# Another table of places for the steps of a fused attention and bilinear feed-forward kernel

## The chip, the cores and the metric

One core of a Trainium2 chip. The metric is the device time of one execution in microseconds (us), the median of several runs; lower is better. The engines are TensorE (PE; its weight loads are shown as PEld), VectorE (DVE), ScalarE (ACT), GpSimd (POOL) and SyncE (SP), which here issues all the transfers. Every engine works through its own queue in the order in which the program was written; semaphores hold an instruction back until what it needs is there, and then everything behind it in that queue waits too.

## The reference

The input x has 2048 rows of 576 numbers; all is float32.

```python
xn = layernorm(x)
qkv = xn @ wqkv                       # 32 heads of 18
s = softmax(mask(q k^T / sqrt(18))) v # a row sees itself and the 255 rows before it
s = concat(s) @ wo
g = silu(((xn @ w_gate) * (xn @ w_up)) @ w_down)   # inner width 4608
return x + s * g
```

## The kernel before

All products run on TensorE in float16, each operand split in a high and a low half (three products in place of one, high-high, high-low, low-high), so "hi" steps (ACT casts), "lo" steps (DVE or POOL subtract) and sums of them make up most of the work of the other engines.

**Before slot 0** (the first 180 us): layernorm, the transposed input XT, then the projections to q, k and v, which go to DRAM.

**The slots.** The feed-forward's inner width is cut into 18 groups g of 256, each worked in four slots: 72 slots in all (`NSLOT`). Slot `4g + 2c + kind` computes gate (kind 0) or up (kind 1) of group g for half c of the rows, by a scheme with seven half-size products in place of eight (`seven_place`, line 1184, PSUM banks named `up`). The seven are taken in the order `ORDER = (0, 2, 1, 3, 4, 5, 6)` and called q0 to q6. Each is read out of its bank by ACT (`seven_copy`, line 1148) or by DVE (`seven_add`, line 1157; `seven_fuse`, line 1151). There are two banks: q1 goes on in q0's after that was read, q3 in q2's, q5 in q3's, q6 in q4's, and the next slot's q0 and q2 take the banks of q5 and q6. So a late read holds TensorE. The scheme needs sums of input blocks (`s_steps`: tiles SX, XD and one block of XT rewritten in place, once at the start) and of weight blocks (`t_sum`, tile `tw`, for each group), all split in halves again.

**Places.** A slot has 16 places; `SEVEN_N` says how many of the 46 products of line 1184 each place has. Between them the program puts all other steps: `at(slot, place, f, ...)` files a step, and after the products of a place its steps are written out in the order in which they were filed (score products first, then `down`). The table `AT` holds the places. A place above 15 lies in the next slot: place 24 of slot 45 is place 8 of slot 46. Negative places lie before slot 0.

**The steps of attention.** There are 64 steps s, each two heads (j) for 512 rows in four blocks of 128 (i). Step s begins in slot b = s + 1 and takes row `b % 4` of the tables `p`, `end` and `en`. For each of n = 2i + j, `AT['p'][b % 4][n]` has five places:

```python
for n in range(8):
    i, j = divmod(n, 2)
    for f, p in zip((score, shifted, probs, turn_probs, weigh), AT["p"][b % NCH][n]):
        at(b, p, f, s, j, i)
at(b, AT["end"][b % NCH][0], finish, s)
at(b, AT["end"][b % NCH][1], finish2, s)
```

- `score` (line 931, DVE): mask and row maximum of a block of scores; the scores themselves are TensorE's (`score_pairs`, line 920, at places 6 and 13).
- `shifted` (line 939, ACT, at j = 1): the factor for the exponent.
- `probs` (lines 943 and 946, ACT): the exponential, and at j = 1 the high halves of both heads in tile `pp`.
- `turn_probs` (line 952): the low half, on DVE where `AT['en'][b % 4][2 + 2i + j]` is 1 and on POOL where it is 0. At j = 1 SP then issues the transposing transfer pp -> pt (line 955) for both heads of the block. Tile pt has three buffers.
- `weigh` (line 964, TensorE): the six products of P and V of one head and block, reading pt into the bank `pv`. The first of the two heads waits for the transfer.
- `finish` (lines 976 and 977, DVE) reads the bank `pv` after the last `weigh` of the step; `finish2` (lines 984 to 992, POOL) scales and splits it; `store_o` sends it to DRAM.

**The other steps of a slot.** `h_hi` and `h_lo` (lines 1025 and 1031, ACT and DVE, places `AT['h']`) split gate times up, in four tiles gv, gt, g and gu; the buffer of gt is taken by the next q0 read, which therefore waits for `h_lo` of gt. `down` (line 1046, bank `dn`, one bank; evicted by DVE, line 1053) is the product with w_down. `ffn_raw`, `ffn_amax` (line 321, ACT), `ffn_spread_*`, `up_hi`/`up_lo`, `dn_*`, `t_*`, `wd_*` load, scale and split the next group's weights. `load_q`, `load_k`, `load_v` (`AT['load']`) fetch the next step's q, k and v. The tables `sx`, `on`, `t0`, `u0`, `g0`, `wd0` place the sums and weight steps of the first group, before and in slots 0 to 2; `on` chooses DVE (1) or POOL (0) for each sum.

**After slot 71** the output projection and the combination with x run in 16 tiles (`o_out`, line 1292).

In what follows a slot's kind is its number modulo 4 (slot 46 is of kind 2), and row r of a table is that of the steps that begin in a slot of kind r.

Of the kernel before, what the change touches and what calls it, by code (L numbers as in the profile page):

```python
# [20 lines left out]
def kernel(  # L21
# [43 lines left out]
    C_OUT = 1.0 / (XS * PROJ * WTOP * WTOP)  # L65
    LEAST, MOST = 2.0 ** -60, 2.0 ** 60

    AT = {'amax': (19, 30, 6),
          'dn': ((45, 45), (48, 55), (54, 49)),
          'down': ((6, 9, 12, 16, 20), (6, 8, 11, 19, 16), (6, 8, 11, 14, 16), (6, 10, 12, 15, 18)),  # L70
          'down_last': ((11, 11, 12, 13, 11), (2, 3, 4, 5, 9)),
          'en': ((0, 1, 0, 0, 0, 0, 1, 1, 0, 0), (0, 1, 0, 0, 0, 1, 1, 0, 0, 0), (1, 1, 0, 0, 0, 0, 1, 1, 0, 0),
                 (0, 1, 0, 0, 0, 0, 0, 1, 0, 0)),
          'end': ((31, 32, 35), (29, 32, 33), (28, 32, 33), (28, 32, 33)),
          'eng': (1, 1, 1, 1, 1, 0, 1, 0, 1, 0, 0, 0, 0, 1),
          'g0': (-22, -17, -22, -18, -10, -16, -14, -11, -11),
          'h': (((17, 20), (15, 16), (17, 21), (19, 20)), ((13, 14), (16, 16), (16, 18), (19, 20))),
          'h_last': ((17, 18), (18, 19)),
          'load': (8, 10, 15),
          'me': (0, 1, 0),  # L80
          'mult': {4: 1, 5: 1, 6: 1},
# [12 lines left out]
          'pairs': (6, 13),  # L94
          'raw': (8, 10, 21, 22, -8, 0),
          'scale': (30, 31, 38, 50),
          'sum': ((46, 52, 55, 56), (64, 66, 67, 70)),
# [5 lines left out]
          't_hi': ((57, 70), (61, 74)),  # L103
          't_lo': ((59, 73), (70, 77)),
          'u0': ((-9, -2, -7, -3), (-7, -2, -6, 3)),
          'up_hi': (41, 54, 45, 60),
          'up_lo': (44, 57, 50, 65),
          'wd': ((58, 72), (65, 73), (71, 78)),
          'wd0': ((-4, 6), (-1, 6), (2, 17))}

    ctx.enter_context(tc.manual_schedule())
    const = ctx.enter_context(tc.tile_pool(name="const", bufs=1))
# [512 lines left out]
    def dn_low(g, k):  # L625
        w = DW[g, k]
        if AT["eng"][4]:
            nc.scalar.activation(w[:, 2], w[:, 0], AF.Copy, scale=1.0 / LO)
# [22 lines left out]
    def at(slot, place, f, *a):  # L651
        todo.setdefault(slot * 16 + place, []).append((f, a))
# [5 lines left out]
    for c in range(NCH):  # L658
        steps = s_steps(c)
        for n, f in enumerate(steps):  # L660
            for k, f in enumerate(f if isinstance(f, tuple) else (f,)):
                at(0, AT["sx"][c][n] + k, f, (nc.gpsimd, nc.vector)[AT["on"][c][n]])
    for k in range(3):
        at(0, AT["g0"][k], ffn_amax, 0, (2, 0, 1)[k])
    for k, f in enumerate((ffn_spread_out, ffn_spread_in, ffn_scale, ffn_scale2)):
        at(0, AT["g0"][5 + k], f, 0)
    for kind in range(2):
        for n in range(4):
            at(0, AT["t0"][kind][n], t_sum, 0, kind, n)
        for pair in range(2):  # L670
            at(0, AT["t0"][kind][4 + pair], t_hi, 0, kind, pair)
            at(0, AT["t0"][kind][6 + pair], t_lo, 0, kind, pair)
# [682 lines left out]
```

## Time and profile before

| what | value |
|---|---|
| runs before | 1584.62 us median of 3 (1583.49 to 1588.78) |
| the profiled execution | 1583.03 us, its span 1581.2 us |
| granted TensorE clock | 1.0 |
| busy: PE, DVE, ACT, POOL | 1549.4, 1267.6, 1047.0, 761.7 us |
| slot 0 begins | 179.53 us after the span's start |
| the last slot begins | 1492.76 us |

The views used below: the page of the whole execution, the list of waits (who waited for whom, in total), the chain of work that ended last in order of time (start, duration, what), and timelines of one engine in a window (start, duration, engine, line, operation, out<-in, shape, count, and in brackets the idle time before it with what ended it). In a timeline equal instructions that follow each other are one row, and the duration of PE rows runs past the next row's start, since matmuls are pipelined and their ends are modelled.

### The profile page before, as it was taken

The page shows a single profiled execution, that of the slowest core. Times are in us where ns is not written, and L with a number is a line of the kernel's source. Part 1 is how long each engine was busy: PE and PEld are TensorE (multiplying, and loading weights), DVE is VectorE, ACT ScalarE, POOL GpSimd, SP SyncE. Part 2 cuts the span into 40 slices and gives each one's busy share as a digit, 9 for nine tenths or more (in the row PEclk, how much of TensorE's full clock was granted, in tenths as well). Part 3 has the DMA queues.
Part 4 walks back from the last instruction along what each step waited for, and adds up shares of the span by engine and source line. Part 5 has one row for each costly group of instructions (what it writes and reads, how often), then busy time and mean ns, then how long its engine had stood idle before and what let it go on. Part 6 is the DMA issues. An engine that isn't in the chain of part 4 may idle for free.

```text
span 1581.2 us, 32793 instructions
## 1 busy us (share of the span) xinstructions
PE 1549.4 (98%) x11898; PEld 769.9 (49%) x11898; DVE 1267.6 (80%) x2803; ACT 1047.0 (66%) x1818; POOL 761.7 (48%) x985
## 2 busy tenths in 40 slices
PE   8999999999999999999999999999999999999999
PEld 5465444444444444444444444444444444444467
DVE  7636788888888989898989898888988888967654
ACT  6534587767777877777877777777877777842130
POOL 4115445545464646464646555655656465622000
PEclk9999999999999999999999999999999999999999
DMA  8683456566557786777777777777786777641238
GB/s 222 208 237 128 147 99 122 107 120 112 110 106 141 129 148 132 140 131 139 138 134 140 130 145 133 145 124 147 136 138 134 135 128 151 126 88 36 65 84 217
DMA packets 566546, 211.67 MB, mean 134 GB/s; under 512 B 504560, under 2 KB 544624, under 8 KB 566384
## 3 DMA queue, kind: packets, MB, share of 16 engines
q1 hardware_dynamic: 566384, 209.58, 65.6%
q8 instruction: 93, 1.52, 0.4%
q14 instruction: 69, 0.57, 0.1%
HBM read 76.63 MB, written 29.00 MB: 67 GB/s over the span
## 4 chain that ended last, share of the span: by engine, by line
PE 73%; DVE 11%; DMA 6%; issue 3%; ACT 2%; POOL 2%; SPq 1%; DVEq 0%; ACTq 0%; POOLq 0%
PE up L1184 33%; PE dn L1046 18%; DMA pt<-pp 5%; PE pv L964 4%; PE s L393 4%; DVE hh L1031 3%; PE up L1134 2%; PE s L1046 2%; PE s L1292 2%; PE s L920 2%; PE up L1292 2%; PE up L393 1%; DVE gt L1160 1%; DVE acc L1053 1%; PE pv L393 1%
## 5 line engine op out<-in xcount | busy, mean ns | idle before, releaser
L1046 PE MATMUL dn<-dnw,hh 128*128 128x512 f16 (+1 forms) x3168 | 442.5, 286 | 0.0
L1046 PEld LDWEIGHTS <-hh 128*128 128x128 f16 x3456 | 222.9, 98 | 224.1 <-issue 21.1
L1053 DVE SCALAR_TENSOR_TENSOR acc<-dn,sc,acc 128x512 f32<-128x512 f32 x310 | 215.3, 694 | 84.2 <-PE dn L1046 82.2
L939 ACT ACTIVATE mx<-mx,sig 128x2 f32<-128x2 f32 x256 | 98.4, 384 | 240.7 <-DVE mx L931 239.5
L1184 PE MATMUL up<-XT,upw 128*128 128x512 f16 x936 | 238.8, 379 | 5.2 <-ACT gt L1148 5.0
L1184 PE MATMUL up<-XT,tw 128*128 128x512 f16 x864 | 232.3, 378 | 4.2 <-DVE gu L1157 1.4
L1184 PE MATMUL up<-sx,tw 128*128 128x512 f16 x864 | 222.9, 378 | 0.1
L1184 PEld LDWEIGHTS <-tw 128*128 128x128 f16 x1728 | 147.4, 97 | 142.6 <-issue 9.1
L519 POOL TENSOR_TENSOR raw<-raw 128x256 f32<-128x256 f32 x140 | 125.1, 894 | 72.6 <-DVE upw L199 63.5
L964 PEld LDWEIGHTS <-pt 128*128 128x128 f16 x2880 | 115.1, 96 | 88.4 <-DMA pt<-pp 22.1
L1184 PEld LDWEIGHTS <-upw 128*128 128x128 f16 x936 | 86.6, 98 | 102.6 <-issue 10.4
L964 PE MATMUL pv<-vt,pt 128*128 128x37 f16 x2880 | 120.5, 179 | 11.4 <-DMA pt<-pp 11.2
L1184 PE MATMUL up<-sx,upv 128*128 128x512 f16 x432 | 111.3, 381 | 0.0
L1160 POOL TENSOR_TENSOR gv<-gv,uv 128x512 f32<-128x512 f32 x36 | 53.5, 1487 | 62.4 <-DVE uv L1157 62.4
L1184 PEld LDWEIGHTS <-upv 128*128 128x128 f16 x576 | 49.2, 97 | 69.4 <-issue 22.1
L321 ACT ACTIVATE upw<-raw 128x1280 bf16<-128x1280 f32 (+1 forms) x51 | 62.3, 1221 | 9.8 <-DMA raw<-in_B_w_up_dram 9.1
L920 PE MATMUL s<-ks,qs 54*128 54x384 f16 (+2 forms) x512 | 60.2, 312 | 0.0
L199 DVE SCALAR_TENSOR_TENSOR tw<-raw,sc,tw 128x512 f16<-128x512 f32 x70 | 57.1, 816 | 0.0
L1160 POOL TENSOR_TENSOR gu<-gu,uu 128x512 f32<-128x512 f32 x36 | 47.5, 1320 | 19.6 <-DVE uu L1157 14.8
L984 POOL TENSOR_TENSOR o<-o,rc 128x144 f32<-128x144 f32 x64 | 29.7, 465 | 56.4 <-DVE o L977 56.4
L1157 DVE SCALAR_TENSOR_TENSOR uu<-up,ut 128x512 f32<-128x512 f32 x36 | 24.9, 692 | 39.6 <-PE up L1134 21.6
L1134 PE MATMUL up<-XT,upv 64*128 64x512 f16 x144 | 55.7, 386 | 0.1
(1356 smaller groups left out, 3234.5 us busy)
## 6 DMA issues: line engine op xcount, KB each, us to landing
raw<-in_B_w_down_dram SPq DMA_DIRECT2D x36, 288.0 KB
qk_d<-qp SPq DMA_DIRECT2D x18, 512.0 KB
raw<-in_B_w_gate_dram SPq DMA_DIRECT2D x36, 256.0 KB
raw<-in_B_w_up_dram SPq DMA_DIRECT2D x36, 256.0 KB
ks<-qk_d SPq DMA_DIRECT2D x96, 81.0 KB
qs<-qk_d SPq DMA_DIRECT2D x128, 54.0 KB
vt<-v_d SPq DMA_DIRECT2D x48, 111.0 KB
qk_d<-qp SPq DMA_DIRECT2D x20, 256.0 KB
```

What stands on the lines that cost most here:

```text
L321: nc.scalar.activation(to[0:src.shape[0], 0:src.shape[-1]], src, AF.Square, accum_out=dst)
L393: nc.tensor.matmul(ps, a, b, start=i == 0 and not opened, stop=i == 12 and opened)
L519: nc.gpsimd.tensor_tensor(to, x0, x1, op=OP.subtract)
L920: nc.tensor.matmul(ps[:, :hi_ - lo_], QS[s][r, i * 128:(i + 1) * 128], KS[s][r, lo_:hi_], start=True, stop=True)
L939: nc.scalar.activation(mx[:, 1], mx[:, 0], AF.Identity, bias=sig[:, 2:3], scale=sig[:, 1:2])
L964: nc.tensor.matmul(PVB[s][:, j, i, :VW], pt[:, nb * j + n + n // nb * nb], VT[s][:, lo_ + n % nb, j * VW:(j + 1) * VW], start=n == 0, stop ...
L1046: nc.tensor.matmul(to, a, b, start=q == 0, stop=q == len(l) - 1)
L1053: nc.vector.scalar_tensor_tensor(d, src, SC[g][:, 9:10], d, op0=OP.mult, op1=OP.add)
L1134: nc.tensor.matmul(CH[q], w, x, start=False, stop=s, skip_group_check=q in ON)
L1160: eng.tensor_tensor(GT[name], GT[name], SV[name], op=OP.mult)
L1184: nc.tensor.matmul(CH[q], a, b, start=CH["first"], stop=last and q not in (1, 2, 5), skip_group_check=q in ON)
L1292: nc.tensor.matmul(pr[j][:, :cols[j].stop - cols[j].start], a, b[:, cols[j]], start=i == 0, stop=i == 13)
```

## The change

Only the table `AT` differs; no step is added or removed. In `p` the places of `weigh` move, with some of `score`, `shifted`, `probs` and `turn_probs` ahead of them; `en` gives one low half in row 0 to POOL and one to DVE, and one in row 1 to POOL; in row 3 `finish` and `finish2` move by two and one places; `load_q` goes three places ahead; some `h`, `up_hi`, `wd`, `t_hi` and `amax` steps move by one to four places; the steps of the first group (`sx`, `on`, `t0`, `u0`, `g0`, `wd0`) get new places and engines, and so do the last slot's `h_last` and `down_last`. Entry 8 of `eng` is read nowhere.

```diff
-    AT = {'amax': (19, 30, 6),
+    AT = {'amax': (21, 30, 6),
...
-          'down_last': ((11, 11, 12, 13, 11), (2, 3, 4, 5, 9)),
-          'en': ((0, 1, 0, 0, 0, 0, 1, 1, 0, 0), (0, 1, 0, 0, 0, 1, 1, 0, 0, 0), (1, 1, 0, 0, 0, 0, 1, 1, 0, 0),
+          'down_last': ((9, 11, 13, 13, 13), (2, 2, 3, 5, 6)),
+          'en': ((0, 1, 0, 0, 0, 0, 0, 1, 0, 1), (1, 1, 0, 0, 0, 0, 1, 0, 0, 0), (1, 1, 0, 0, 0, 0, 1, 1, 0, 0),
                  (0, 1, 0, 0, 0, 0, 0, 1, 0, 0)),
-          'end': ((31, 32, 35), (29, 32, 33), (28, 32, 33), (28, 32, 33)),
-          'eng': (1, 1, 1, 1, 1, 0, 1, 0, 1, 0, 0, 0, 0, 1),
-          'g0': (-22, -17, -22, -18, -10, -16, -14, -11, -11),
-          'h': (((17, 20), (15, 16), (17, 21), (19, 20)), ((13, 14), (16, 16), (16, 18), (19, 20))),
-          'h_last': ((17, 18), (18, 19)),
-          'load': (8, 10, 15),
+          'end': ((31, 32, 35), (29, 32, 33), (28, 32, 33), (30, 33, 33)),
+          'eng': (1, 1, 1, 1, 1, 0, 1, 0, 0, 0, 0, 0, 0, 1),
+          'g0': (-22, -17, -22, -17, -12, -15, -14, -12, -11),
+          'h': (((17, 19), (15, 15), (17, 21), (18, 19)), ((13, 14), (16, 16), (16, 21), (19, 21))),
+          'h_last': ((17, 18), (19, 19)),
+          'load': (8, 7, 15),
...
-          'on': ((0, 0, 0, 1, 1, 1, 1, 1, 0, 1, 0, 0, 0, 0, 1, 0, 1),
-                 (0, 0, 0, 1, 1, 0, 0, 0, 0, 0, 1, 0, 1, 1, 0, 0, 1),
-                 (1, 1, 0, 1, 0, 0, 1, 0, 0, 0, 1, 1, 1, 0, 1, 1, 1),
-                 (0, 0, 1, 0, 0, 0, 0, 1, 0, 0, 1, 1, 1, 1, 0, 1, 1)),
-          'p': (((6, 7, 8, 11, 21), (6, 7, 10, 12, 22), (7, 8, 9, 13, 22), (7, 8, 10, 13, 23), (13, 14, 15, 18, 24),
-                 (13, 14, 15, 18, 24), (13, 15, 20, 21, 30), (15, 17, 20, 21, 30)),
-                ((6, 7, 8, 11, 22), (6, 7, 8, 12, 25), (7, 8, 12, 13, 22), (8, 8, 12, 15, 23), (13, 14, 15, 18, 24),
-                 (13, 14, 16, 20, 24), (17, 17, 20, 21, 27), (17, 17, 20, 21, 28)),
-                ((6, 6, 7, 8, 22), (6, 6, 7, 10, 22), (7, 9, 14, 15, 22), (7, 9, 14, 15, 23), (13, 15, 15, 17, 26),
-                 (13, 14, 15, 19, 26), (14, 15, 20, 21, 28), (15, 17, 20, 21, 28)),
-                ((6, 7, 8, 11, 22), (6, 7, 8, 12, 22), (7, 8, 12, 13, 22), (7, 8, 12, 13, 23), (13, 14, 15, 19, 26),
-                 (13, 14, 15, 21, 26), (13, 17, 20, 21, 28), (15, 17, 20, 21, 28))),
+          'on': ((0, 0, 0, 1, 0, 1, 1, 1, 0, 0, 0, 0, 0, 1, 1, 0, 1),
+                 (0, 0, 1, 1, 1, 0, 0, 0, 1, 0, 1, 0, 1, 1, 0, 1, 1),
+                 (1, 1, 1, 1, 0, 0, 1, 0, 0, 0, 1, 1, 1, 0, 1, 1, 0),
+                 (0, 1, 1, 0, 0, 0, 0, 0, 0, 0, 1, 0, 0, 1, 0, 1, 0)),
+          'p': (((6, 7, 8, 11, 22), (6, 7, 10, 13, 22), (6, 8, 9, 13, 23), (7, 8, 10, 13, 23), (13, 13, 14, 17, 27),
+                 (13, 13, 14, 18, 27), (13, 18, 21, 22, 30), (18, 18, 21, 22, 30)),
+                ((6, 7, 8, 11, 22), (6, 7, 10, 12, 22), (7, 10, 12, 15, 22), (10, 10, 14, 15, 23), (13, 15, 16, 18, 26),
+                 (13, 15, 16, 20, 26), (16, 18, 19, 20, 28), (17, 18, 19, 20, 28)),
+                ((6, 6, 7, 8, 22), (6, 6, 7, 12, 22), (7, 8, 14, 15, 22), (7, 8, 14, 15, 23), (13, 14, 15, 17, 26),
+                 (13, 14, 15, 19, 26), (14, 17, 18, 21, 28), (15, 17, 18, 21, 28)),
+                ((6, 7, 8, 11, 20), (6, 7, 8, 12, 20), (7, 8, 12, 13, 22), (7, 8, 12, 13, 22), (13, 14, 15, 19, 26),
+                 (13, 14, 15, 21, 26), (13, 17, 20, 21, 30), (17, 17, 20, 21, 30))),
...
-          'sx': ((-24, -24, -24, -23, -22, -22, -18, -18, -17, -17, -14, -13, -13, -20, -20, -17, -14),
-                 (-21, -21, -21, -18, -17, -17, -16, -14, -14, -11, -10, -10, -9, -15, -15, -15, -12),
-                 (-14, -11, -11, -10, -7, -7, -4, -3, 2, 3, 6, 6, 6, 2, 17, 17, 18),
-                 (-4, -2, -1, 5, 8, 12, 12, 14, 14, 16, 20, 26, 27, 23, 26, 26, 30)),
-          't0': ((-19, -9, -7, -7, -6, -6, -4, -3), (0, 2, 4, 6, 5, 11, 9, 11)),
-          't_hi': ((57, 70), (61, 74)),
+          'sx': ((-24, -22, -22, -22, -21, -21, -18, -15, -15, -15, -14, -14, -13, -20, -19, -17, -14),
+                 (-21, -21, -21, -20, -17, -17, -16, -14, -14, -14, -13, -12, -9, -16, -15, -12, -12),
+                 (-14, -8, -8, -8, -7, -7, -4, -3, -3, 2, 6, 6, 6, -1, 15, 20, 20),
+                 (-2, -1, -1, 5, 8, 12, 12, 14, 16, 19, 23, 35, 38, 25, 26, 33, 35)),
+          't0': ((-20, -9, -7, -7, -6, -6, -4, -3), (0, 2, 5, 6, 5, 11, 9, 15)),
+          't_hi': ((57, 70), (59, 75)),
...
-          'u0': ((-9, -2, -7, -3), (-7, -2, -6, 3)),
-          'up_hi': (41, 54, 45, 60),
+          'u0': ((-9, -2, -9, -3), (-7, -2, -6, -2)),
+          'up_hi': (39, 54, 47, 60),
...
-          'wd': ((58, 72), (65, 73), (71, 78)),
-          'wd0': ((-4, 6), (-1, 6), (2, 17))}
+          'wd': ((58, 72), (66, 77), (72, 78)),
+          'wd0': ((-4, 6), (-1, 6), (5, 19))}
```

## The prediction

> **What bounds the kernel now.** I read the page first, then the list of waits, then the chain of work that ended last, and then timelines around the waits.
>
> ```profile
> span 1581.2 us, 32793 instructions
> PE 1549.4 (98%) x11898; PEld 769.9 (49%) x11898; DVE 1267.6 (80%) x2803; ACT 1047.0 (66%) x1818; POOL 761.7 (48%) x985
> PEclk9999999999999999999999999999999999999999
> ```
>
> TensorE is busy 98% of the span at the full granted clock, and its work does not change. So the change can only fill, or open, holes in TensorE's queue. The list of waits names them:
>
> ```profile
> PE pv L964 <- DMA pt<-pp: 11.2, 15, 2.3
> PE up L1184 <- ACT gt L1148: 5.0, 17, 1.6
> ```
>
> Products of P and V wait 11.2 us, in 15 places, for the transposing transfer. The chain gives the same from another side. Every fourth slot has the same stretch of 18 products, so their distances are periods of four slots (start, duration, what):
>
> ```profile
> 522.60 3.89 PE up L1184 x18
> ...
> 749.70 3.88 PE up L1184 x18
> 824.35 3.88 PE up L1184 x18
> ...
> 1354.95 3.88 PE up L1184 x18
> ```
>
> From 522.60 to 1354.95 lie 11 periods, 75.67 us each; one without such a wait takes 824.35 - 749.70 = 74.65. Eleven times 1.02 is 11.2 us: in the middle of the kernel the variable part is these waits.
>
> **Term 1: `weigh` in row 1.** The timeline of PE in slot 46 (kind 2), and the two largest rows of their sort:
>
> ```profile
> 1041.18 0.47 PE L964 MATMUL pv<-vt,pt 128*128 128x37 f16 x12 [0.42 <-DMA pt<-pp]
> 1041.49 0.59 PE L1184 MATMUL up<-XT,tw 128*128 128x512 f16 x2
> 1041.92 0.38 PE L1184 MATMUL up<-sx,tw 128*128 128x512 f16 x1
> 1042.30 1.24 PE L1184 MATMUL up<-sx,tw 128*128 128x512 f16 x5
> ...
> 890.78 0.47 PE L964 MATMUL pv<-vt,pt 128*128 128x37 f16 x12 [1.72 <-DMA pt<-pp]
> 1269.96 0.47 PE L964 MATMUL pv<-vt,pt 128*128 128x37 f16 x12 [2.28 <-DMA pt<-pp]
> ```
>
> The first is block 2 of a step of row 1: low half at place 20, product at 24, four places apart, the closest pair of the table. It moves to 26. What then lies between is the rest of place 8, the three products of place 9 and the two of place 10: five products, 0.216 us each (3.88/18), so 1.08 us later. The bracket understates a hole by about 0.16 us, because the 0.38 us of a product run past its 0.216. The waits outside kind 0 sum to 8.2 us in ten rows by their brackets (11.2 less the 3.0 of term 2), 9.8 with the 0.16 each. Left over are what exceeds 1.08: 0.8 and 1.36 of the two largest, some 0.1 of the next, 2.3 in all. Term 1 is -7.5 (0 if the transfer comes later by as much, -9.8 if none is left). Does it come later? POOL gets one more low half in row 1 (i1, j1), but ahead of `finish2`, for which POOL waits anyway; the transfer itself follows POOL's (i2, j1), whose predecessors are as before. Block 3 leaves place 27 for 28. Its transfer stands behind block 2's in SP's queue and needs a buffer of pt, freed at place 22 by block 0 (25 before); `store_o` and the loads behind it gain, and `load_q`, which passes `load_k` and one `ffn_raw` on that queue, finds its buffer free since the slot before. Both at nothing.
>
> **Term 2: `weigh` in row 3, block 2.** Its places stay, 21 and 26, five apart; what changes is DVE's queue ahead of the low half.
>
> ```profile
> 1156.05 0.47 PE L964 MATMUL pv<-vt,pt 128*128 128x37 f16 x12 [0.99 <-DMA pt<-pp]
> 1073.17 1.01 DVE L1031 SCALAR_TENSOR_TENSOR hh<-hh,g 128x512 f16<-128x512 f16 x1
> 1074.10 1.21 DVE L1031 SCALAR_TENSOR_TENSOR hh<-hh,gu 128x512 f16<-128x512 f16 x1
> 1075.23 0.55 DVE L952 TENSOR_TENSOR pp<-sm__14852,pp 128x384 f16<-128x384 f32 x1
> 1075.85 3.27 SPq L955 DMA_TRANSPOSE pt<-pp  x2
> ```
>
> SP issues right after DVE's low half, and the two `h_lo` (g, gu) that stood ahead of it go behind: 1075.23 - 1073.17 = 2.06 us earlier. The largest wait of this sort is the 0.99 shown; five of them, 0.16 to 0.99, sum to 3.0 by brackets, 3.8 with the 0.16. Term 2 is -3.8 (0 to -3.8). The delayed `h_lo` feed `down` a slot later: nothing.
>
> **Term 3: the q0 read in kind 0.** Nearly all of the 17 waits for ACT gt are in slots of kind 0, such as slot 48:
>
> ```profile
> 1070.53 0.54 DVE L931 CUSTOM_DVE_ANT_0 sm__14856<-s,bias 128x384 f32<-128x384 f32 x1
> 1071.00 0.85 DVE L1031 SCALAR_TENSOR_TENSOR hh<-hh,gt 128x512 f16<-128x512 f16 x1
> 1071.94 0.60 ACT L1148 ACTIVATE gt<-up 128x512 f32<-128x512 f32 x1 [1.05 <-DVE hh L1031]
> 1072.59 1.67 PE L1184 MATMUL up<-XT,upw 128*128 128x512 f16 x7 [0.22 <-ACT gt L1148]
> ...
> 1080.15 0.69 DVE L1157 SCALAR_TENSOR_TENSOR gv<-up,gt 128x512 f32<-128x512 f32 x1
> 1080.95 1.03 PE L1184 MATMUL up<-XT,tw 128*128 128x512 f16 x4
> ```
>
> The `score` ahead of `h_lo` of gt moves behind it, 0.54 us, more than the 0.22 + 0.16 waited. But DVE has no idle time from here to the read at 1080.15, whose end at 1080.84 releases q5 at 1080.95, and up to that read it does the same steps in another order. What q1 gains, q5 waits: -0.5 in all (0 to 12 x 0.38 = -4.6).
>
> **Term 4: `finish` in row 3, against the change.**
>
> ```profile
> 1083.97 0.20 DVE L976 RECIPROCAL rc<-pv 128x8 f32<-128x8 f32 x1
> 1084.58 0.69 DVE L1157 SCALAR_TENSOR_TENSOR gt<-up,gt 128x512 f32<-128x512 f32 x1
> 1088.11 0.69 DVE L1157 SCALAR_TENSOR_TENSOR gu<-up,gu 128x512 f32<-128x512 f32 x1
> 1088.91 1.46 PE L1184 MATMUL up<-sx,tw 128*128 128x512 f16 x6
> ```
>
> Now `finish` (0.61 us, 1083.97 to 1084.58) fills the time in which DVE would wait for q5, whose products end at about the same moment. At place 30 it follows the q5 read, ahead of the q6 read, and that one's end (1088.80) releases q2 of the next slot at 1088.91. Three scores, two low halves and the read lie between without idle time, so the read comes up to 0.6 us later. Two of these DVE steps now run beside `finish2` on POOL, which will come later too; I take 0.35 per group in the 12 groups from slot 20 on and a trifle before: +4.3 (0 to 16 x 0.6 = +9.6). ACT's `wd_hi` of 0.39 us ahead of the exponentials there meets idle time.
>
> The Trainium skill ("SBUF — State Buffer", Who interferes with whom) says that a DVE instruction with two SBUF inputs and a GpSimd one that reads SBUF exclude each other for a whole instruction. The `h_lo` row of 1.21 us in term 2 agrees, against this one beside an idle POOL:
>
> ```profile
> 1036.55 0.68 DVE L1031 SCALAR_TENSOR_TENSOR hh<-hh,g 128x512 f16<-128x512 f16 x1
> ```
>
> By that rule the new order in term 3's stretch could cost or save one such difference, 0.5 us, in each group, 6 us either way; the sum takes none.
>
> **Term 5: slots 0 to 2.** The waits of PE from 179 to 226 us:
>
> ```profile
> PE up L1184 <- ACT gt L1148: 1.6, 1, 1.6
> PE up L1184 <- DVE gu L1157: 1.4, 2, 0.9
> PE up L1184 <- DVE uu L1157: 1.2, 1, 1.2
> PE up L1184 <- DVE gv L1157: 1.1, 1, 1.1
> ...
> 183.40 0.61 DVE L199 SCALAR_TENSOR_TENSOR upv<-raw,sc,upv 128x384 f16<-128x384 f32 x1
> 208.02 1.49 DVE L952 TENSOR_TENSOR pp<-sm__2061,pp 128x256 f16<-128x256 f32 x1
> ```
>
> With two of 0.2 that is 5.7 us, nearly all for DVE's reads. DVE loses the `up_lo` of 0.61 (now before slot 0, where it idles) and the low half of 1.49 (to POOL), and a sum. Against that the third block of the first sums (z, split at places 35 and 36) is needed by q3 at 39, and its tail goes out at 39 for place 45. I take -2.5 (-6 to +3). The earlier places before slot 0 meet a TensorE that waits for almost nothing there, and the last slot's new places move products within a full queue: nothing.
>
> The rest is covered: `up_hi`, `wd_hi`, `t_hi` and `amax` move by a few places to where their results are needed later still, and row 0's last low half on DVE (place 22) has its product at 30.
>
> **The sum.** -7.5 - 3.8 - 0.5 + 4.3 - 2.5 = -10.0 us. From the profiled execution's 1583.0 (its span of 1581.2 and 1.8 around it) that is 1573.0; the median of the runs is 1.6 above that execution, which I leave inside the range.
>
> **Rivals.**
>
> *More of it, 1567.* `finish` falls into a pause (term 4 at 0) and the early slots gain more: -7.5 - 3.8 - 0.5 - 4 = -16. For it: groups with a wait of term 2 have slack before that q2 now. Against it: no idle bracket in term 4's DVE rows.
>
> *The waits move on, 1583.* The transfers come as much later as the products: block 2's of row 1 needs POOL, and SP may stand at a transfer that waits for its buffer. Then terms 1 and 2 shrink to -3, term 4 stays. Against it: the order on POOL and SP. The table also does not do all that its name says: block 2 of row 3 keeps five places, of row 1 gets six; were term 2 alone missing, the time would be 1577, within the forecast.
>
> *Slower, 1591: ACT holds q1 in kind 2.* Row 1's exponentials go from places 12 and 15 to 14 and 16, right ahead of the q0 read at place 17.
>
> ```profile
> 1029.26 0.39 ACT L939 ACTIVATE mx<-mx,sig 128x2 f32<-128x2 f32 x1 [2.57 <-DVE mx L931]
> 1033.39 0.59 ACT L1148 ACTIVATE gt<-up 128x512 f32<-128x512 f32 x1
> 1034.42 1.67 PE L1184 MATMUL up<-XT,upw 128*128 128x512 f16 x7
> ```
>
> That read ends at 1033.98, 0.44 us ahead of q1. Were it 1.5 us later, as long as a moved exponential with its copy, 1.06 us would be lost in each of 17 slots, 18 us: +8. It decides from 0.44 + 10/17 = 1.0 us on. Against it: ACT idles 2.57 us just before, and `amax`, which now follows that row, can go into that gap.
>
> **How the numbers follow.** Forecast 0.51 (1573, own range 1568 to 1578), more of it 0.18, waits move on 0.20, slower 0.11. The range is 1563 to 1585: below by what terms 3 and 5 could add, above to the waits that move on; the slower rival and the outer tails stay out. A change under 0.3% (4.8 us; the runs shown span 5.3) can't be told from none: faster 0.72 from the first two and a little of the third, same 0.17, slower 0.11.
>
> **What the next profile would show.** Term 1: waits of pv for the transfer under 3 us, periods of four slots under 75.2. Term 2: none in kind 0. Term 3: the waits for ACT gt gone, q5 at the end of DVE's read. Term 4: a new row, PE up waits for DVE's q6 read in slots of kind 1, about 0.3 us each. Term 5: under 4 us of waits before 226 us. I would be wrong if a wait for ACT appeared in kind 2, or if the pv waits stood as they are.

## The result and the profile after

| kernel | runs | median us (range) | ratio to before, 95% interval |
|---|---|---|---|
| before | 4 | 1586.16 (1583.49 to 1588.78) | |
| changed | 4 | 1574.11 (1572.70 to 1575.38) | 0.9924 [0.9902, 0.9946] |

The change is 12.0 us faster by the medians. The two profiled executions lie closer together, 1583.03 and 1575.38 us: that of before lies below all four of its runs, that of the changed kernel is the highest of its four. Of the 46 runs of the kernel before that stand beside the experiments, the 22 with a granted clock of 1.0 have a median of 1582.8 us and the 24 with 0.997 to 0.999 one of 1586.7, while all four runs of the changed kernel had 1.0. Like for like the change is thus worth 8 to 9 us, near the difference of the two profiled executions, which both had 1.0. The page of the changed kernel, which answers to the first rows of the prediction:

```profile
span 1573.3 us, 32759 instructions
...
PE 1550.6 (99%) x11898; PEld 770.8 (49%) x11898; DVE 1273.1 (81%) x2790; ACT 1050.7 (67%) x1818; POOL 759.4 (48%) x998
...
PEclk9999999999999999999999999999999999999999
```

TensorE's work is the same and its clock too, so the 7.9 us by which the span is shorter are holes. The list of waits (us in total, times, longest):

```profile
PE up L1184 <- ACT gt L1148: 4.5, 17, 1.1
PE pv L964 <- DMA pt<-pp: 2.9, 4, 1.1
PE up L1184 <- DVE gu L1157: 2.7, 8, 0.9
```

The products of P and V wait 2.9 us where they waited 11.2. The row of 5.0 us for ACT's read of gt has hardly moved (its 0.5 us are one early wait, 1.6 to 1.1), and the row for DVE's reads into gu, 1.4 us before, has grown. The chain, with the same stretch of 18 products once in four slots:

```profile
518.51 3.88 PE up L1184 x18
...
668.48 3.88 PE up L1184 x18
743.59 3.88 PE up L1184 x18
818.44 3.88 PE up L1184 x18
...
1346.86 3.88 PE up L1184 x18
```

Eleven periods are 828.35 us, 75.30 each (75.67 before). But one without a wait for a transfer is now 74.85 (818.44 - 743.59) or 75.11 (743.59 - 668.48), where it was 74.65. So something was paid for the gain. Last, the waits of TensorE from 179 to 226 us:

```profile
PE up L1184 <- DVE gu L1157: 1.7, 2, 0.9
PE up L1184 <- ACT gt L1148: 1.1, 1, 1.1
PE up L1184 <- DVE uu L1157: 0.6, 1, 0.6
PE up L1184 <- DVE gv L1157: 0.4, 1, 0.4
```

For the accounts below a wait is measured as the distance from the start of one product to that of the next, less the usual distance of that pair; this sees the 0.16 us that the brackets leave out. By the starts of slots, the span changed by -2.3 us up to slot 4, by -1.8 from slot 4 to 20, by -4.0 from slot 20 to 64, by +0.5 from there to slot 71 and by -0.3 after it: -7.9. The -4.0 of the middle are, for slots 20 to 63, three numbers: waits for transfers 11.2 to 3.0 us, new waits for the q3 read ahead of q5 at place 12 of kind 0 (+2.1), and for the q6 read at place 2 of kind 1 (+2.2).

### The profile page after: what moved, and what is told of

It reads as the page before. It is cut to its first block, busy times and chain, and to the rows that moved or that the text cites. A ratio compares the mean times of both kernels' runs of the same rounds, so it can differ in the third digit from the quotient of the medians.

```text
span 1573.3 us, 32759 instructions
## 1 busy us (share of the span) xinstructions
PE 1550.6 (99%) x11898; PEld 770.8 (49%) x11898; DVE 1273.1 (81%) x2790; ACT 1050.7 (67%) x1818; POOL 759.4 (48%) x998
## 4 chain that ended last, share of the span: by engine, by line
PE 70%; DVE 9%; POOL 8%; issue 6%; ACT 3%; DMA 2%; SPq 0%; DVEq 0%; POOLq 0%; ACTq 0%
PE up L1184 32%; PE dn L1046 18%; POOL pp L952 4%; PE pv L964 3%; PE s L393 3%; PE up L1134 2%; PE s L1046 2%; DVE hh L1031 2%; DMA pt<-pp 2%; PE s L1292 2%; PE s L920 2%; PE up L1292 2%; PE up L393 1%; POOL raw L519 1%; DVE gt L1160 1%
## 5 line engine op out<-in xcount | busy, mean ns | idle before, releaser
L1184 PEld LDWEIGHTS <-tw 128*128 128x128 f16 x1728 | 152.0, 97 | 161.7 <-issue 14.6
L519 POOL TENSOR_TENSOR raw<-raw 128x256 f32<-128x256 f32 x140 | 121.4, 867 | 57.1 <-DVE upw L199 48.2
L964 PEld LDWEIGHTS <-pt 128*128 128x128 f16 x2880 | 109.3, 96 | 64.9 <-DMA pt<-pp 5.8
L964 PE MATMUL pv<-vt,pt 128*128 128x37 f16 x2880 | 112.9, 180 | 2.9 <-DMA pt<-pp 2.9
L984 POOL TENSOR_TENSOR o<-o,rc 128x144 f32<-128x144 f32 x64 | 34.4, 537 | 71.2 <-DVE o L977 71.2
L1134 PE MATMUL up<-XT,upw 64*128 64x512 f16 x144 | 55.7, 387 | 0.0
```

The source lines that it names most:

```text
L519: nc.gpsimd.tensor_tensor(to, x0, x1, op=OP.subtract)
L964: nc.tensor.matmul(PVB[s][:, j, i, :VW], pt[:, nb * j + n + n // nb * nb], VT[s][:, lo_ + n % nb, j * VW:(j + 1) * VW], start=n == 0, stop ...
L1134: nc.tensor.matmul(CH[q], w, x, start=False, stop=s, skip_group_check=q in ON)
L1184: nc.tensor.matmul(CH[q], a, b, start=CH["first"], stop=last and q not in (1, 2, 5), skip_group_check=q in ON)
```

## Experiments

All times below are medians of six runs (eight for the second), each set beside runs of the kernel before on the same chip; four chips were used, so kernels of different groups are compared by their ratios and by their traces, and a difference of medians between such kernels is only a rough figure. Each ratio holds the difference of clock named above. An interval of a ratio is some 0.0036 wide, 5.7 us; what is smaller rests on the waits in the traces.

| kernel | median us (range) | ratio to before, 95% interval |
|---|---|---|
| row 1 weigh alone | 1576.99 (1575.03 to 1578.49) | 0.9943 [0.9926, 0.9960] |
| row 3 low halves alone | 1579.98 (1578.53 to 1583.11) | 0.9972 [0.9954, 0.9990] |
| changed, finish back | 1571.20 (1570.16 to 1571.74) | 0.9906 [0.9890, 0.9922] |
| changed, old start | 1576.71 (1575.09 to 1578.85) | 0.9944 [0.9925, 0.9963] |
| changed, row 1 block 2 at 28 | 1575.86 (1574.70 to 1578.75) | 0.9942 [0.9923, 0.9961] |
| changed, score back | 1573.14 (1572.45 to 1574.17) | 0.9924 [0.9907, 0.9940] |
| changed, finish2 late | 1572.61 (1572.12 to 1573.69) | 0.9921 [0.9904, 0.9937] |
| first combination | 1571.27 (1570.66 to 1575.73) | 0.9916 [0.9898, 0.9934] |
| changed, gt and ut in turn | 1570.32 (1569.18 to 1574.10) | 0.9915 [0.9899, 0.9932] |
| second combination | 1571.60 (1571.22 to 1571.92) | 0.9919 [0.9906, 0.9932] |
| third combination | 1570.35 (1569.27 to 1572.13) | 0.9912 [0.9898, 0.9926] |
| fourth combination | 1567.33 (1565.96 to 1569.18) | 0.9896 [0.9880, 0.9912] |

### The parts of the change, one at a time

Row 1's weigh places in the table of before:

```diff
 row 1:  block 0, second head   (6, 7, 8, 12, 25)    -> (6, 7, 8, 12, 22)
         block 2, both heads    (..., 24)            -> (..., 26)
         block 3, first head    (17, 17, 20, 21, 27) -> (17, 17, 20, 21, 28)
```

> The kernel before with one edit: in row 1 the four late weigh places are those of the changed table (block 2 at 26 instead of 24, block 3 at 28 for both heads, one product of block 0 at 22 instead of 25). Theory (the holes are the distance between low half and product): 6.8 us faster than before, ratio 0.9957; the waits of pv for the transfer in slots of kind 2 fall from 10.6 us (by excess over the usual spacing) to 2.3 to 3.7, the 3.85 us in kind 0 stay. Rival (the table works as a whole, the transfers come later when the products do, and single moves shift the waits): less than 3 us faster, with waits of pv in kind 2 above 7 us or new waits for the evictions in kind 2.

Measured: 7.9 us faster than before by the medians, 6.6 by the spans of the profiled executions (1581.2 and 1574.6). In the list of waits of this kernel, where the row for ACT gt is as before:

```profile
PE pv L964 <- DMA pt<-pp: 6.2, 10, 1.1
```

By the finer account the waits of pv in kind 2 go from 10.6 to 4.5 us and those in kind 0 stay at 3.9; nothing else moves. The theory holds, and its rival falls: the moved products alone do it.

The low halves of g and gu in row 3 (`h`, second set), in the table of before:

```diff
-          'h': (..., ((13, 14), (16, 16), (16, 18), (19, 20))),
+          'h': (..., ((13, 14), (16, 16), (16, 21), (19, 21))),
```

> The kernel before with one edit: the low halves of the feed-forward's tiles g and gu that are worked in kind 3 and 0 go from places 18 and 20 to 21 and 21, behind the low half of P of row 3's block 2 on DVE. Theory (the transfer in kind 0 waits for DVE's queue alone): 3.8 us faster than before, ratio 0.9976, no wait of pv in kind 0, the ten waits in kind 2 as before. Rival (the transfer is held elsewhere, by SP or by its buffer, or the later low halves delay DVE's read for q5): 1 us or less, with waits for DVE's reads in kind 0 grown by what pv gained.

Measured: 4.9 us faster by the medians. Its list of waits:

```profile
PE pv L964 <- DMA pt<-pp: 11.0, 10, 2.4
...
PE up L1184 <- DVE gu L1157: 2.5, 6, 0.9
```

None of the ten waits is in kind 0, where there were 3.9 us by the finer account. That the total is still 11.0 is kind 2, whose waits are the old table's and were longer in this execution (12.7 us against 10.6), so the profiled execution is one of the longer ones of the eight (1582.51). In the waits, term 2 is as large as said, and it is DVE's queue. A price showed at once: 0.8 us more for gu in early groups.

The changed kernel with row 3's block 3 and finish where they were:

```diff
-          'end': (..., (30, 33, 33)),
+          'end': (..., (28, 32, 33)),
 row 3, block 3: weigh 30 -> 28, both heads
```

> The changed kernel with row 3's block 3 and finish back at places 28 and 28, finish2 at 32 and the store at 33, as in the kernel before. Theory (finish ahead of the q6 read holds q2 of kind 1): 2.5 us faster than the changed kernel, 1571.6 us; the 2.5 us of waits for gu at place 2 of kind 1 gone. Rival A (the 0.3 us in every other group come from the GpSimd instruction beside the read, not from finish itself): the gain is as large, since both go away together, so this run alone does not tell them apart. Rival B (finish ahead of the q5 read delays that one, as DVE has no idle time): no gain or a loss up to 2 us, with waits for DVE's q5 read at the start of kind 1.

Measured: 2.9 us below the changed kernel's median. The 2.5 us at place 2 of kind 1 are gone, the waits at place 12 of kind 0 stay at 2.8, the rest is 1.0 us less of pv. Theory and rival A agree with it; rival B is out.

The changed kernel with the six tables of the first group as before (`sx`, `on`, `t0`, `u0`, `g0`, `wd0`):

> The changed kernel with the six tables of the first group (first sums, weight steps before and in slots 0 to 2) of the kernel before. Theory (the spread of these steps is worth what slot 3 began earlier): 2.3 us slower than the changed kernel, 1576.4 us, all of it before slot 3. Rival (the start-up follows from slots' steps outside these tables, such as the low half of P in row 0 that went to GpSimd): within 0.7 us of the changed kernel.

Measured: 2.6 us above the changed kernel. Slot 3 starts at 226.36 us, as before the change (226.28; 224.02 after it). Term 5 lies in these tables. Together, the four parts by their medians are -7.9 - 4.9 - 2.6 + 2.9 = -12.5 us against the -12.0 measured. That they come so close is partly luck: each is known to some 3 us either way, the first two both hold the difference of clock, and the new waits at place 12 of kind 0 are not among them. The account that adds up is that of the waits in the traces.

### Why the wait for ACT's read of gt stayed

The score was moved behind the low half of gt, and yet the q0 read came no sooner. The timeline of the changed kernel in slot 48, DVE, GpSimd and ACT:

```profile
1063.91 0.74 DVE L1053 SCALAR_TENSOR_TENSOR acc<-dn,sc,acc 128x512 f32<-128x512 f32 x1
1064.57 1.32 DVE L1031 SCALAR_TENSOR_TENSOR hh<-hh,gt 128x512 f16<-128x512 f16 x1
1065.81 0.55 DVE L931 CUSTOM_DVE_ANT_0 sm__14858<-s,bias 128x384 f32<-128x384 f32 x1
...
1066.29 0.61 DVE L199 SCALAR_TENSOR_TENSOR upv<-raw,sc,upv 128x384 f16<-128x384 f32 x1
...
1064.07 1.27 POOL L1160 TENSOR_TENSOR gu<-gu,uu 128x512 f32<-128x512 f32 x1
...
1065.98 0.60 ACT L1148 ACTIVATE gt<-up 128x512 f32<-128x512 f32 x1 [1.02 <-DVE hh L1031]
```

GpSimd's multiplication ends at 1065.34, and the low half, begun at 1064.57, ends 0.55 us later. It was 0.85 us long before, behind the score. The test puts the score back, and nothing else:

```diff
-  row 3, block 3, second head: (17, 17, 20, 21, 30)
+  row 3, block 3, second head: (15, 17, 20, 21, 30)
```

> The changed kernel with the second head's score of row 3's block 3 back at place 15, ahead of the low half of tile gt on DVE, where it stood before. Theory (that low half ends when GpSimd's multiplication of tile gu ends, whatever stands ahead of it, since the two exclude each other): the waits for ACT gt in kind 0 stay at 5.9 us in all, the low half of gt measures 0.85 us again instead of 1.32, DVE gains about 0.47 us behind it and the 2.8 us of waits for its read at place 12 of kind 0 fall to about 1.2: 1.6 us faster than the changed kernel, 1572.5 us. Rival (the prediction's own sum, in which the score costs its 0.54 us on the way to the q0 read): the waits for ACT gt grow by 0.47 us in 12 to 16 groups, 5.6 us or more slower, 1579.7 us.

Measured: 1.0 us below the changed kernel, with the same ratio, so not told apart from it. The waits for ACT gt stay at 6.0 us and those at place 12 of kind 0 at 2.8. Its timeline at the same point:

```profile
1062.79 0.54 DVE L931 CUSTOM_DVE_ANT_0 sm__14858<-s,bias 128x384 f32<-128x384 f32 x1
...
1063.26 0.85 DVE L1031 SCALAR_TENSOR_TENSOR hh<-hh,gt 128x512 f16<-128x512 f16 x1
1064.03 1.08 DVE L199 SCALAR_TENSOR_TENSOR upv<-raw,sc,upv 128x384 f16<-128x384 f32 x1
...
1062.28 1.27 POOL L1160 TENSOR_TENSOR gu<-gu,uu 128x512 f32<-128x512 f32 x1
1063.52 1.17 POOL L519 TENSOR_TENSOR raw<-raw 128x256 f32<-128x256 f32 x1
```

The low half is 0.85 us again and still ends 0.55 us after GpSimd's multiplication, in each of the eleven groups from slot 20 to 63, as in the kernel before (0.85 us) and the changed one (1.32 us). The prediction's own sum (5.6 us slower) is refuted. The theory's second half failed too: the 0.47 us that DVE saved were taken by the next step, the low half of a weight block, 1.08 us in place of 0.61, held by GpSimd's next instruction. So DVE's time in these two steps is set by where GpSimd's instructions end, whatever the order of its own.

What the wait was worth is seen when the read needs no low half. Gate's and up's tiles are taken in turn, each at a time when the other is free:

```diff
-        GT[name] = post.tile([128, 512], F32, name="g" + name, bufs=1)
+        GT[name] = post.tile([128, 512], F32, name=("u" if name == "t" and TF["c"] else "g") + name, bufs=1)
...
-        SV[name] = post.tile([128, 512], F32, name="u" + name, bufs=1)
+        SV[name] = post.tile([128, 512], F32, name=("g" if name == "t" and TF["c"] else "u") + name, bufs=1)
```

(`TF["c"]` is the half of the rows that the slot works on.)

> The changed kernel in which the q0 read of a slot of kind 2 goes into the tile of ut (free there since place 14 of the slot before), and that of kind 3 into the one of gt, in turn, so that no q0 read waits for the low half of gt; no memory is added. Theory (the prediction's: DVE has no idle time up to the read that releases q5): the 5.9 us of waits for ACT gt in kind 0 fall below 1, those at place 12 of kind 0 for DVE's read grow from 2.8 by nearly as much, and the time is within 1.5 us of the changed kernel, 1573.0 us. Rival (DVE's chain itself starts from that q0 read): waits at place 4 go and those at place 12 stay at 2.8, 5 us faster, 1569.1 us.

Measured: 3.8 us below the changed kernel by the medians and 1.4 by the ratios, so the time alone does not choose between the two. The list of waits:

```profile
PE up L1184 <- DVE gu L1157: 4.2, 9, 0.9
PE pv L964 <- DMA pt<-pp: 1.8, 2, 1.1
```

The row for ACT gt is gone; its early wait of 1.1 us now has the name ut. By the finer account kind 0 lost 5.9 us at place 4 and 0.5 at place 12 and got 4.4 at place 7, where q3 waits for DVE's q2 read: 2.0 us net, nearer to the theory. The theory named the right engine and the wrong place: the read that comes next in DVE's queue collects the debt. The rest lies in the waits of pv and of place 2 in kind 1, which the edit does not touch and which were 2.5 us shorter in this execution.

### What the 0.31 us of term 4 are

The wait for the q6 read stands in eight of the twelve groups from slot 20 on, 0.31 us each, and in the others it is under 0.05. Slot 45 of the changed kernel has it and slot 41 has not:

```profile
930.97 0.35 DVE L199 SCALAR_TENSOR_TENSOR upw<-raw,sc,wd 64x128 f16<-64x128 f32 x1
931.35 0.69 DVE L1157 SCALAR_TENSOR_TENSOR gu<-up,gu 128x512 f32<-128x512 f32 x1
...
931.01 0.59 POOL L984 TENSOR_TENSOR o<-o,rc 128x144 f32<-128x144 f32 x1 [1.78 <-DVE o L977]
...
1005.37 0.41 DVE L977 TENSOR_REDUCE o<-pv 128x144 f32<-128x288 f32 x1
1005.81 0.62 DVE L199 SCALAR_TENSOR_TENSOR upw<-raw,sc,wd 64x128 f16<-64x128 f32 x1
1006.47 0.69 DVE L1157 SCALAR_TENSOR_TENSOR gu<-up,gu 128x512 f32<-128x512 f32 x1
...
1005.86 0.43 POOL L984 TENSOR_TENSOR o<-o,rc 128x144 f32<-128x144 f32 x1 [1.78 <-DVE o L977]
```

`finish` releases two instructions at the same moment: DVE's next one, a small weight step, and GpSimd's first of `finish2`. In slot 41 DVE takes 0.35 us and GpSimd 0.59, in slot 45 0.62 and 0.43: one of them runs first and the other waits for it. To test this, `finish2` goes behind GpSimd's next low half, `store_o` follows it, and `finish` stays:

```diff
-          'end': (..., (30, 33, 33)),
+          'end': (..., (30, 37, 38)),
```

> The changed kernel with finish2 of row 3 at place 37 instead of 33, behind GpSimd's next low half; finish stays at place 30. Theory (the 0.31 us in every other group come from the small weight step of DVE, 0.35 us alone and 0.62 beside GpSimd's first instruction of finish2): that step measures 0.35 us in every group, the waits for gu at place 2 of kind 1 fall from 2.5 us to under 0.7, 1.9 us faster than the changed kernel, 1572.2 us. Rival (finish itself, 0.61 us on DVE, holds the q6 read in those groups): the waits stay at 2.5 us and the time within 0.7 us of the changed kernel.

Measured: 1.5 us below the changed kernel by the medians, 0.5 by the ratios, both within the noise; the waits decide. The row of the weight step is now the same in each of the eleven groups:

```profile
1004.13 0.35 DVE L199 SCALAR_TENSOR_TENSOR upw<-raw,sc,wd 64x128 f16<-64x128 f32 x1
```

and the waits at place 2 of kind 1 fall from 2.5 us to none. So `finish` at place 30 costs TensorE next to nothing by itself (it used up the slack: slots of kind 1 are 18.57 us, 18.53 before); the price came from the GpSimd instruction that it releases.

### Where the rest of term 1 went when it was pushed further

The changed kernel with block 2 of row 1 two places later still:

```diff
-  row 1, block 2: (13, 15, 16, 18, 26), (13, 15, 16, 20, 26)
+  row 1, block 2: (13, 15, 16, 18, 28), (13, 15, 16, 20, 28)
```

> The changed kernel with block 2's products of P and V in row 1 at place 28 instead of 26, for both heads. Theory (what is left of term 1 is the same distance once more): the 3.7 us of waits of pv at place 10 of kind 2 are covered by the products and evictions in between and go, 3.7 us faster than the changed kernel, 1570.4 us; the run-to-run spread narrows too, since no product stands close behind a transfer in these slots. Rival (the waits move on): block 3's products at place 28, or finish at 29, come late in their turn and 2 us or more of waits stand at place 12 of kind 2 or at the next slot's start.

Measured: 1.8 us above the changed kernel. No product of P and V waits at block 2 or 3 any more, but `down` waits 5.4 us at place 11 of kind 2 for its eviction: 0.32 us in each of eleven groups from slot 18 on and 1.7 in slot 46. First slot 42, one of the eleven, then slot 46:

```profile
958.85 0.67 DVE L452 TENSOR_REDUCE sc<-upv 128x3 f32<-128x384 f32 x1
...
961.84 1.46 PE L1046 MATMUL dn<-dnw,hh 128*128 128x512 f16 x6 [0.15 <-DVE acc L1053]
...
1035.37 0.71 DVE L452 TENSOR_REDUCE sc<-upv 128x3 f32<-128x384 f32 x1 [1.28 <-DMA upv<-sd_f]
...
1037.61 0.75 DVE L1053 SCALAR_TENSOR_TENSOR acc<-dn,sc,acc 128x512 f32<-128x512 f32 x1
...
1030.36 0.33 SPq L447 DMA_DIRECT2D upv<-sd_f  x1
...
1038.40 1.45 PE L1046 MATMUL dn<-dnw,hh 128*128 128x512 f16 x6 [1.57 <-DVE acc L1053]
```

In slot 42 no step is late: `down`'s products start 13.17 us after the slot's start, as in the changed kernel. There the twelve products of P and V, 0.31 us, stood ahead of them at place 10 and filled the time in which the bank was still being read; now they stand behind, at place 12, and the same time is a wait. So where no transfer had been late, the edit costs this time: such a slot is 20.14 us long, 19.84 in the changed kernel. Slot 46 is another matter. DVE stands at the reduction of the weight maxima (`ffn_scale`, place 38) for another transfer, issued 5 us earlier, and the eviction stands behind it. In the changed kernel's slot 46 that reduction waits 0.98 us too, hidden under the wait of pv: two transfers were late at one place, and the list named only the first. The rival "the waits move on" held, by mechanisms that neither text had named.

Three combinations followed. The first: this edit, finish back, score back, and the low half of the small weight tile of kind 0 at 73 in place of 72 (`wd`).

> The changed kernel with five edits: block 2 of row 1 at 28, block 3 and finish of row 3 back at 28, the second head's score of row 3's block 3 back at place 15, and the low half of the small weight tile of kind 0 at place 73 instead of 72, behind DVE's q3 read in kind 0. Theory (the single gains add up, as they lie in different slots): 2.9 + 3.7 + 1.6 + 0.6 = 8.8 us faster than the changed kernel, 1565.3 us. Rival (they share DVE's queue of kind 0, where a gain ahead of one read is waited out at the next): 6.6 us or less, with waits for ACT gt or for DVE's q5 read in kind 0 grown.

Measured: 1571.27, 2.8 us below the changed kernel where the sum of the single gains was 8.8. The edit of `wd` took the waits at place 12 of kind 0 from 2.8 to 0.6 us, finish back took its 2.5; `down`'s 4.5 us stayed, 0.3 us in each group with products of P and V moved behind it and 0.9 in slot 46. The second leaves the score and moves the reduction behind that eviction:

```diff
-          'scale': (30, 31, 38, 50),   'up_hi': (39, 54, 47, 60),
+          'scale': (30, 31, 40, 50),   'up_hi': (41, 54, 47, 60),
```

> The changed kernel with block 2 of row 1 at 28, block 3 and finish of row 3 back at 28, the small weight tile's low half of kind 0 at 73, and the group's weight scales (DVE's reduction of the maxima that a transfer spreads) at place 40 instead of 38, the first weight cast that needs them at 41 instead of 39. Theory (the waits of down for its eviction at place 11 of kind 2 are DVE standing at that reduction for the transfer, 1.28 us in slot 46): with the reduction behind the eviction they go, 4.5 us less than the kernel with the first five edits, 1566.8 us. Rival (the wait moves on once more): the reduction now holds DVE's q3 or q4 read of kind 2, waits for gv at place 12 of kind 2 of 3 us or more, time 1570 us or above.

Measured: 1571.60. `down`'s waits are gone, since the eviction no longer stands behind the reduction and starts a microsecond earlier, and 5.5 us stand at place 12 of kind 2, 0.46 us in each of twelve groups ahead of q5. Slot 46:

```profile
1034.01 0.17 DVE L454 TENSOR_SCALAR sc<-sc 128x3 int32<-128x3 int32 x1
...
1034.42 0.85 DVE L456 TENSOR_SCALAR sc<-sc 128x3 int32<-128x3 int32 x1
1035.19 0.68 DVE L1157 SCALAR_TENSOR_TENSOR gv<-up,gt 128x512 f32<-128x512 f32 x1
...
1034.34 1.78 POOL L952 TENSOR_TENSOR pp<-sm__14445,pp 128x384 f16<-128x384 f32 x2 [3.76 <-ACT pp L946]
...
1035.92 1.02 PE L1184 MATMUL up<-XT,tw 128*128 128x512 f16 x4 [0.30 <-DVE gv L1157]
```

An operation on 128x3 numbers, 0.17 us alone, takes 0.85 and holds the q3 read, since it meets GpSimd's low half (two of them in the row of 1.78 us). The rival held: it had named this wait, and the theory missed that the step would move into GpSimd's way. The third adds the tiles taken in turn:

> The kernel of the row before (five table edits) with the tiles of gt and ut taken in turn as well. Theory (DVE's queue of kind 0 has 0.2 us to give per group since the small low half left it): the waits for ACT gt in kind 0 fall below 1 us from 5.9, those at place 12 of kind 0 grow to 2 to 3, 2.5 us faster than without, 1564.3 us. Rival (all of it is waited out at place 12): within 0.7 us.

Measured: 1570.35, 1.25 us less than the second: between theory and rival, with the waits at place 7 as in the kernel with the tiles in turn alone (6.6 us). The last drops what kind 2 did not repay (block 2 stays at 26, the reduction at 38) and keeps finish back, `wd` at 73 and the tiles in turn:

> The changed kernel with block 3 and finish of row 3 back at 28, the small weight tile's low half of kind 0 at 73, and the tiles of gt and ut taken in turn; block 2 of row 1 stays at 26 and the reduction at 38. Theory (the gains in kinds 0 and 1 hold side by side, and in kind 2 the waits of pv are the cheapest of the three forms seen): waits in kind 0 fall from 12.1 to 8.3 us as in the kernel before it, those at place 2 of kind 1 from 2.5 to 0, those of pv stay at 2 to 3.7: 6.3 us faster than the changed kernel, 1567.8 us, and below every other kernel of the study. Rival (the earlier slots of kind 1 and 0 bring the transfers' products of kind 2 closer, and pv takes the gain): 1570 us, with waits of pv of 5 us or more.

Measured: 1567.33, near the 1567.8 expected and the lowest median of all, ratio 0.9896 [0.9880, 0.9912] where the changed kernel has 0.9924 [0.9902, 0.9946]. The intervals still overlap; the spans of the profiled executions are 1564.2 and 1573.3 us. Kind 0 waits some 8 us, place 2 of kind 1 none, and pv 0.9.

## Why the prediction was right, and where it was not

The time was forecast at 1573.0 and is 1574.1; the signs of the large terms were right, and the errors of the smaller ones partly cancel. By the traces the working comes out as follows.

*Term 1*, -7.5: measured -6.8; the edit on its own shows the cause, with -6.1 in the same waits. What is left, 3.7 us, stands in five groups at place 10 of kind 2, 0.2 to 1.2 us each; the forecast left 2.3. The step that was a little off is the size of the largest lateness of a transfer, taken from one execution.

*Term 2*, -3.8: measured -3.9, none left in kind 0, shown by the edit on its own. The rows that answer to those of before, from the changed kernel's slot 48:

```profile
1067.21 0.88 DVE L952 TENSOR_TENSOR pp<-sm__14854,pp 128x384 f16<-128x384 f32 x1
1068.01 1.21 DVE L1031 SCALAR_TENSOR_TENSOR hh<-hh,g 128x512 f16<-128x512 f16 x1
1069.14 0.68 DVE L1031 SCALAR_TENSOR_TENSOR hh<-hh,gu 128x512 f16<-128x512 f16 x1
1069.93 0.69 DVE L1157 SCALAR_TENSOR_TENSOR gu<-up,gt 128x512 f32<-128x512 f32 x1
```

*Term 3*, -0.5: wrong; measured +2.2. The step that failed is "moves behind it, 0.54 us, more than the 0.22 + 0.16 waited". The end of that low half is set by GpSimd, and putting the score back changed nothing. The prediction had this rule before it (the Trainium skill, "SBUF — State Buffer", Who interferes with whom: a DVE instruction with two SBUF inputs and a GpSimd one that reads SBUF shut each other out for a whole instruction), priced it at 0.5 us a group, and took none. The rows agree with the rule: the low half grew by 0.47 us in every group, the very time that the move had freed. It should have been applied to the one row on which the term rested. The second half of the step, that q5 would collect what q1 gains, was right in kind, and q5 waits 0.19 us more in each group though q1 gained nothing. The q2 read of the kernel before, in the same slot:

```profile
1075.70 0.68 DVE L1157 SCALAR_TENSOR_TENSOR gu<-up,gt 128x512 f32<-128x512 f32 x1
```

From the end of the eviction in kind 0's first place to this read were 5.17 us (1070.53 to 1075.70) and are now 5.36 (1064.57 to 1069.93). Here the low half of gu stands right ahead of a read that writes the same tile, 0.79 us from start to start. But that is not enough for the wait: the kernel with row 3's low halves alone has the same order and the same 5.36 us (1073.17 to 1078.53), and no wait at place 12 from slot 20 on. Below are slot 48 of the changed kernel and then of that one:

```profile
1069.19 1.47 PE L1046 MATMUL dn<-dnw,hh 128*128 128x512 f16 x6
1070.69 0.75 DVE L1053 SCALAR_TENSOR_TENSOR acc<-dn,sc,acc 128x512 f32<-128x512 f32 x1
...
1077.49 1.47 PE L1046 MATMUL dn<-dnw,hh 128*128 128x512 f16 x6
1078.53 0.69 DVE L1157 SCALAR_TENSOR_TENSOR gu<-up,gt 128x512 f32<-128x512 f32 x1
1079.14 0.74 DVE L1053 SCALAR_TENSOR_TENSOR acc<-dn,sc,acc 128x512 f32<-128x512 f32 x1
```

The eviction starts 0.76 us after the read in the one and 0.61 in the other, because `down`'s products end later, at 1070.66. The table moves block 0 of row 3 from place 22 to 20, and its twelve products now stand ahead of `down`'s. The q3 read comes later by both. The prediction has no word on this move. The two reasons are read from the traces, and neither was tested by itself; moving the small `wd` step out of the way removed the wait.

*Term 4*, +4.3: the place and the size of one wait were right (0.3 at place 2 of kind 1), the sum is 2.5, since it stands in two groups of three, and the cause was another. Not the 0.61 us of `finish` but the collision with `finish2`, shown by the late `finish2`. The prediction saw that GpSimd would run beside DVE there and used it only to lower its estimate.

*Term 5*, -2.5: measured -2.3 by slot 4, shown by the old tables.

*Rivals.* "More of it" needed term 4 at nothing; it cost 2.5. "The waits move on" was priced at 1583; by its own terms, from the 1583.0 of the forecast, it is 1581.3 (-3 - 0.5 + 4.3 - 2.5). It did not come for the products of P and V in this table, but other waits came as soon as block 2 went two places further. "Slower" needed ACT late at q1 of kind 2; no such wait appeared in the slots after the first three.

*What the next profile should show.* Waits of pv under 3 us: 2.9. Periods under 75.2: 75.30, missed, for the two new waits. None in kind 0: so. Waits for ACT gt gone: wrong. A new row of 0.3 us in kind 1: there. Under 4 us before 226 us: 3.8.

The terms as measured, -6.8 - 3.9 + 2.2 + 2.5 - 2.3, with +0.4 for gu in early groups and -0.3 after slot 71, make -8.2, the profiled pair's span -7.9. So the forecast sum of -10.0 was too good for the pair that it was made against: 1573.0 stands against a profiled execution of 1575.38. That the forecast time came nearer to the median, 1574.1, is luck, since that profiled execution is the highest of the four runs.

## What to carry to other kernels

Ask of a moved step not only how long its row is, but which row of the other engine ends with it: a DVE step that ends a fixed time after a GpSimd instruction gains nothing from being issued earlier. Before moving products away from a late transfer, ask what they fill where they stand: here twelve of them filled the 0.31 us that the next products had to wait for their bank, and in groups where no transfer was late the move only turned work into a wait. The list of waits names only the releaser that came last, so a second late transfer at the same place does not show. Where every read of an engine is just in time, a gain at one of them is collected at the next, so sum the waits of the whole slot and not those of one place.

## What the runs showed of the hardware

The exclusion of DVE and GpSimd is exact: in eleven of eleven groups of all fourteen kernels the low half of gt ended 0.55 us after GpSimd's multiplication, and its duration was 0.85 or 1.32 us only by when it was issued. Two instructions issued 0.05 us apart swapped who waits from group to group (0.35 and 0.59 us, or 0.62 and 0.43). That even DVE's operation on 128x3 integers with one input goes from 0.17 to 0.85 us was not expected (0.85 to 0.87 in each of twelve groups); the same section of the Trainium skill says that one-input operations such as `tensor_scalar` can enter, under conditions on their operands, a mode that takes both ports and then contend. The row agrees, and no run shows which mode it was. Operations that read PSUM and one SBUF input kept their time beside GpSimd (the score 0.55, the eviction 0.73 to 0.75 us).

What sets the spread of the runs is open. All 50 runs of the kernel before lie within 12.6 us, four of the changed kernel within 2.7 and six of the second combination, whose products of P and V do not wait, within 0.7. But the third combination, where they do not wait either, spreads by 2.9, and the changed kernel with finish back, where they wait 2.7 us, by 1.6; the numbers of runs and the granted clock differ too.
